# A gated mix of a spectral filter and a state-space layer: the spectral part moves into the matmul accumulation

## The chip, the cores and the metric

The kernel runs on one core of one Trainium2 chip. The metric is device time in microseconds (us). Three runs of the kernel before gave 412.79, 413.42 and 415.82 us, so the median is 413.42 us.

The core has five engines that run their own queues in order and wait for each other on semaphores: PE multiplies matrices into PSUM, DVE (vector) and ACT (scalar) work elementwise and read PSUM, POOL is hardly used here, and SP issues the transfers (DMAs).

## The reference

For x of 2048 rows by 1024 columns, with a gate g per row:

```
g = sigmoid((x * gate_w).sum(-1))
a = irfft2(rfft2(x) * (w_r + 1j*w_i))               # spectral part
b = 2*Re(C h) + x*Dskip,  h_t = Lam_bar h_{t-1} + B_bar x_t   # state-space part
out = g*a + (1-g)*b
```

The gate and `1-g` are rounded to bf16, and the output is bf16.

## The kernel before, in words

The output is made in 16 row tiles of 128 rows (`tb`). The state-space part works in 8 chunks of 256 rows (`c`), each in two halves of the state (`q`); such a half is a **unit** (L202). A unit multiplies x by B on PE (two blocks `psu` of 32 matmuls, L209), ACT casts each block into the tile `h` (L211), and DVE rotates, scans (L223) and rotates back (L215 to L234). The unit leaves `h` ready for the **C product** (`c_gemm`, L456): for a row tile, 16 matmuls of 512 columns from `h` (L462) and 4 small ones that add x*Dskip (L466), once for each half of the columns, into a tile `ps_y` of two PSUM banks.

The spectral part (`gfnet`, L240) runs between the units until about half of the span and leaves `ZT`. What is left of it for a row tile stands in `finish` (L477): 8 matmuls (L483) into `ps_id`, one ACT instruction that scales them by g into a piece of the buffer `raw` (L486), and four DVE additions and subtractions (L488, L489, L491, L492) that give g*a in a tile `ga`. Then DVE multiplies `ps_y` by 1-g and adds `ga` (L500), and SP sends the tile out (L501).

The first four row tiles have their C product done before the spectral part is ready. `early` (L470) scales it by 1-g on ACT and sends it to the scratch tensor `y_scratch` in two halves. `finish` without a `psy` fetches it again: for each half a load into the one buffer `yl` (L497) and a DVE addition (L498). These are the **late tiles** 0 to 3. The twelve others are own tiles 4 to 15.

The main loop (L663) makes chunks 4 to 7. Each of its 8 **halves** is a unit, the C product and `finish` of an own tile two chunks back, and, in the first four halves, `finish` of a late tile. After the loop the own tiles 12 to 15 remain (L670); this is the **tail**.

PSUM is full: two buffers of two banks for `ps_y` (pool `psA`), and two of two banks that `psu` and `ps_id` share (pool `psU`). The piece of `raw` that ACT writes is chosen by `tb % 2`, and so is the piece that L488 and L489 write. The tiles `ga` have two buffers. The scheduler reorders the program a little when it writes each engine's queue; on the chip the queues are strictly in order.

Of the kernel before, what the change touches and what calls it, by code (L numbers as in the profile page):

```python
# [11 lines left out]
ACT = mybir.ActivationFunctionType  # L12
ALU = mybir.AluOpType
FP32 = mybir.dt.float32
# [6 lines left out]
D = 1024  # L21
K = 512
H = K // 2
P = 128
# [60 lines left out]
def kernel(  # L85
# [17 lines left out]
    nc = tc.nc  # L103
    x = A_x[0]
    out2 = out[0]
# [15 lines left out]
    y_dram = dram.tile([NEARLY, 2, P, K], FP32, name="y_scratch")  # L121


    cpool = ctx.enter_context(tc.tile_pool(name="cpool", bufs=1, side="left"))
# [18 lines left out]
    ident = cpool.tile([P, P], BF16, name="ident")  # L143
# [53 lines left out]
    def halloc(shape, dtype):  # L197
        pool = hpool[hcount[0] % (NHA + NHB) >= NHA]
        hcount[0] += 1
        return pool.tile(shape, dtype, name="h")  # L200

    def unit(c, q):  # L202
        sh = [P, 2, 4, TC]
        u = halloc(sh, BF16)
        for ri in range(2):
            psu = psU.tile([P, 4, TC], FP32, name="psu", tag="psu")
            for j in range(4):
                for d8 in range(8):
                    nc.tensor.matmul(psu[:, j, :], lhsT=BT[4 * q + j][:, ri, d8, :],  # L209
                                     rhs=xT[:, d8, TC * c:TC * (c + 1)], start=(d8 == 0), stop=(d8 == 7))  # L210
            nc.scalar.copy(out=u[:, ri], in_=psu)  # L211
        js = slice(4 * q, 4 * q + 4)
        bc = lambda i: tab[:, i:i + 1, js, :].to_broadcast(sh)
        su = up.tile(sh, BF16, name="su")
        nc.vector.tensor_mul(out=su, in0=u[:, ::-1], in1=bc(1))  # L215
        nc.vector.tensor_mul(out=u, in0=u, in1=bc(0))  # L216
        nc.vector.tensor_add(out=u[:, 0], in0=u[:, 0], in1=su[:, 0])  # L217
        nc.vector.tensor_sub(out=u[:, 1], in0=su[:, 1], in1=u[:, 1])  # L218
        if c:
            nc.vector.tensor_add(out=u[:, :, :, 0], in0=u[:, :, :, 0], in1=carry[:, :, js])  # L220
        for ri in range(2):
            seg = u[:, ri].rearrange("p j t -> p (j t)")
            nc.vector.tensor_tensor_scan(out=seg, data0=rz[:, js].rearrange("p j t -> p (j t)"), data1=seg,  # L223
                                         initial=0.0, op0=ALU.mult, op1=ALU.add)
        if c + 1 < NCH:
            gl = u[:, :, :, TC - 1]
            nc.vector.tensor_mul(out=ck[:, 0, :, js], in0=gl, in1=cTC[:, js].unsqueeze(1).to_broadcast([P, 2, 4]))
            nc.vector.tensor_mul(out=ck[:, 1, :, js], in0=gl[:, ::-1], in1=sTC2[:, :, js])
            nc.vector.tensor_add(out=carry[:, :, js], in0=ck[:, 0, :, js], in1=ck[:, 1, :, js])
        sg = up.tile(sh, BF16, name="sg", tag="su")  # L230
        nc.vector.tensor_mul(out=sg, in0=u[:, ::-1], in1=bc(3))  # L231
        nc.vector.tensor_mul(out=u, in0=u, in1=bc(2))  # L232
        nc.vector.tensor_add(out=u[:, 0], in0=u[:, 0], in1=sg[:, 0])  # L233
        nc.vector.tensor_sub(out=u[:, 1], in0=u[:, 1], in1=sg[:, 1])  # L234
        hs[c, q] = u


    fft = {}
# [196 lines left out]
    def pull(budget):  # L435
        state["credit"] += budget
        while state["credit"] > 0 and not state["done"]:
            try:
                v = next(gen)
                if v == "ia":  # L440
                    after_ia()
                elif v == "ib":
                    after_ib()
                else:
                    state["credit"] -= v
            except StopIteration:
                state["done"] = True
# [5 lines left out]
            nc.sync.dma_start_transpose(out=CT[ri][:, :, P * q:P * (q + 1)], in_=src[P * q:P * (q + 1), :])  # L453


    def c_gemm(tb, pool=None, tag="ps"):  # L456
        c, tq = tb // 2, tb % 2
        psy = (pool or psA).tile([P, D], FP32, name="ps_y", tag=tag)
        for dh in range(2):
            for i in range(16):  # L460
                jb, ri = i // 2, i % 2
                nc.tensor.matmul(psy[:, 512 * dh:512 * (dh + 1)], lhsT=hs[c, jb // 4][:, ri, jb % 4, P * tq:P * (tq + 1)],  # L462
                                 rhs=CT[ri][:, jb, 512 * dh:512 * (dh + 1)], start=(i == 0), stop=False)
            for d4 in range(4):
                d8 = 4 * dh + d4
                nc.tensor.matmul(psy[:, P * d8:P * (d8 + 1)], lhsT=xT[:, d8, P * tb:P * (tb + 1)],  # L466
                                 rhs=fft["dgD"][:, d8, :], start=False, stop=(d4 == 3))
        return psy

    def early(tb):  # L470
        psy = c_gemm(tb, psU, "psu")
        for hf in range(2):
            ye = fft["gq"].tile([P, K], FP32, name="ye", tag="ga")
            nc.scalar.activation(out=ye, in_=psy[:, K * hf:K * (hf + 1)], func=ACT.Copy, scale=omg[:, tb:tb + 1])
            nc.sync.dma_start(out=y_dram[tb, hf], in_=ye)

    def finish(tb, psy=None):  # L477
        ZT_t = fft["ZT"]
        pse = psU.tile([P, 4, H], FP32, name="ps_id", tag="psu")
        for slot, (cls, ri) in enumerate(((0, 0), (1, 1), (0, 1), (1, 0))):  # L480
            for kb in range(2):
                i = 4 * cls + 2 * kb + ri
                nc.tensor.matmul(pse[:, slot, :], lhsT=ZT_t[:, i, tb, :], rhs=fft["Gi"][:, i, :],  # L483
                                 start=(kb == 0), stop=(kb == 1))
        part = raw[:, D * (2 + tb % 2):D * (3 + tb % 2)].rearrange("p (s c n) -> p s c n", s=2, c=2)
        nc.scalar.activation(out=part.rearrange("p s c n -> p (s c) n"), in_=pse, func=ACT.Copy, scale=gB[:, tb:tb + 1])  # L486
        eo = raw[:, D * (4 + tb % 2):D * (5 + tb % 2)].rearrange("p (c k) -> p c k", c=2)
        nc.vector.tensor_add(out=eo[:, :, 0:H], in0=part[:, 0], in1=part[:, 1])  # L488
        nc.vector.tensor_sub(out=eo[:, :, K - 1:H - 1:-1], in0=part[:, 0], in1=part[:, 1])  # L489
        ga = fft["gq"].tile([P, 2, K], BF16, name="ga")  # L490
        nc.vector.tensor_add(out=ga[:, 0], in0=eo[:, 0], in1=eo[:, 1])  # L491
        nc.vector.tensor_sub(out=ga[:, 1], in0=eo[:, 0], in1=eo[:, 1])  # L492
        o = ga.rearrange("p h n -> p (h n)")
        if psy is None:
            for hf in range(2):
                ye = fft["gq"].tile([P, K], FP32, name="yl", bufs=1)
                nc.sync.dma_start(out=ye, in_=y_dram[tb, hf])  # L497
                nc.vector.tensor_add(out=ga[:, hf], in0=ye, in1=ga[:, hf])  # L498
        else:
            nc.vector.scalar_tensor_tensor(out=o, in0=psy, scalar=omg[:, tb:tb + 1], in1=o, op0=ALU.mult, op1=ALU.add)  # L500
        nc.sync.dma_start(out=out2[P * tb:P * (tb + 1), :], in_=o)  # L501


    def turn_x(r):
# [71 lines left out]
    for r in range(16):  # L576
        if r >= 2:
            turn_x(r)
        for d8 in range(8):
            nc.tensor.matmul(zps[:, r:r + 1], lhsT=xT[:, d8, P * r:P * (r + 1)], rhs=gwT[:, d8:d8 + 1],  # L580
                             start=(d8 == 0), stop=(d8 == 7))
# [12 lines left out]
    raw = t3p.tile([P, 6 * D], BF16, name="raw")  # L594
# [38 lines left out]
    gB = cpool.tile([P, 16], FP32, name="gB")  # L633
    nc.vector.tensor_copy(out=gB, in_=g_bf)
    omg_bf = cpool.tile([P, 16], BF16, name="omg_bf")
    nc.vector.tensor_scalar(out=omg_bf, in0=g_bf, scalar1=-1.0, scalar2=1.0, op0=ALU.mult, op1=ALU.add)
    omg = cpool.tile([P, 16], FP32, name="omg")
    nc.vector.tensor_copy(out=omg, in_=omg_bf)
    pull(5.0)
    unit(0, 0)  # L640
    pull(7.5)
# [19 lines left out]
    todo = list(range(NEARLY, 16))  # L661
    late = list(range(NEARLY))
    for c in range(4, 8):  # L663
        for q in range(2):
            unit(c, q)
            tb = todo.pop(0)
            finish(tb, c_gemm(tb))
            if late:
                finish(late.pop(0))
    for tb in todo:  # L670
        finish(tb, c_gemm(tb))


# [28 lines left out]
```

## Time and profile before

| what | value |
|---|---|
| time of the three runs, median | 413.42 us |
| time of the profiled execution | 413.43 us |
| its span, first to last instruction | 411.6 us |
| busy PE, DVE, ACT in the span | 365.1, 307.8, 168.9 us |
| mean granted TensorE clock | 0.953 of full speed |

The profile is one execution. Its rows give times from the start of the span. A row "PE ... x32" is a run of instructions put together; the time in brackets is how long the engine stood idle before it, and what ended the wait. Matmuls are pipelined, so the rate of PE is read from the starts of two rows, not from the duration of one instruction.

### The profile page before, as it was taken

The numbers are of one execution on the slowest core, as the hardware profiler recorded it, in microseconds if no ns is written. First come the engines' busy times: TensorE is split into PE (matmuls) and PEld (weight loads), VectorE is DVE, ScalarE is ACT, GpSimd is POOL, SyncE is SP. The second block draws the span as 40 slices with busy tenths as digits, with TensorE's granted clock in tenths as the row PEclk, the third lists the DMA queues.
The fourth block names the chain that finished last, engine by engine and source line by source line (L and its number), as shares of the span: only waits on it lengthen the run. The fifth ranks groups of instructions, "written<-read, shape, count | busy, mean of one in ns | idle before, by whom it ended". The sixth has DMA issues, their size and how long they took to land. (4 is left out here: it accounts for less than half of the span.)

```text
span 411.6 us, 6481 instructions
## 1 busy us (share of the span) xinstructions
PE 365.1 (89%) x2601; PEld 239.7 (58%) x2601; DVE 307.8 (75%) x477; ACT 168.9 (41%) x210; POOL 28.8 (7%) x68
## 2 busy tenths in 40 slices
PE   4868998999797998999999988689796999999992
PEld 4836555667574454457766765556464767764551
DVE  2873598196989898990098897959696999999332
ACT  2759797664221588848721212121212113202111
POOL 7600011162000000000000000000000000000000
PEclk9879999999899699999999999969898999999997
DMA  7999921987742288659310103011111000000001
GB/s 207 340 201 208 212 77 53 223 191 148 179 146 79 82 274 314 225 173 292 123 53 2 51 2 100 3 51 51 53 51 53 25 27 2 25 27 16 36 32 45
DMA packets 58077, 45.84 MB, mean 111 GB/s; under 512 B 38720, under 2 KB 43200, under 8 KB 57792
## 3 DMA queue, kind: packets, MB, share of 16 engines
q1 hardware_dynamic: 57616, 45.41, 38.8%
q0 software_dynamic: 352, 0.02, 0.7%
q8 instruction: 20, 0.33, 0.3%
q14 instruction: 9, 0.07, 0.1%
q10 hardware_dynamic: 80, 0.01, 0.0%
HBM read 22.35 MB, written 14.69 MB: 90 GB/s over the span
## 5 line engine op out<-in xcount | busy, mean ns | idle before, releaser
L209 PE MATMUL psu<-xT,BT 128*128 128x256 bf16 x1024 | 129.3, 283 | 14.8 <-ACT raw L486 13.4
L209 PEld LDWEIGHTS <-BT 128*128 128x128 bf16 x1024 | 103.1, 101 | 38.8 <-issue 15.8
L462 PE MATMUL ps_y<-CT,h 128*128 128x512 bf16 x512 | 117.2, 379 | 0.7 <-DVE ga L500 0.7
L462 PEld LDWEIGHTS <-h 128*128 128x128 bf16 x512 | 49.5, 98 | 53.2 <-issue 0.9
L223 DVE TENSOR_TENSOR_SCAN h<-rz,h 128x1024 bf16<-128x1024 f32 x32 | 71.8, 2278 | 0.3
L486 ACT ACTIVATE raw<-ps_id,gB 128x1024 bf16<-128x1024 f32 x16 | 17.8, 1113 | 109.1 <-PE ps_id L483 85.5
L215 DVE TENSOR_TENSOR su<-h,tab 128x2048 bf16<-128x2048 bf16 x16 | 19.6, 1222 | 48.6 <-ACT h L211 48.5
L211 ACT CAST h<-psu 128x1024 bf16<-128x1024 f32 x32 | 32.3, 1010 | 57.1 <-PE psu L209 57.1
L249 PE MATMUL ps_fd<-G_sb,preT 128*128 128x512 bf16 x128 | 32.0, 397 | 4.7 <-ACT X L252 4.3
L249 PEld LDWEIGHTS <-preT 128*128 128x128 bf16 x128 | 18.6, 146 | 15.2 <-issue 8.5
L252 ACT CAST X<-ps_fd 128x1024 bf16<-128x1024 f32 x16 | 20.7, 1304 | 9.3 <-PE ps_fd L249 9.3
L359 ACT CAST X<-ps_s 128x1024 bf16<-128x1024 f32 x16 | 16.2, 1013 | 17.1 <-PE ps_s L357 17.1
L216 DVE TENSOR_TENSOR h<-h,tab 128x2048 bf16<-128x2048 bf16 x16 | 19.6, 1222 | 0.5
L488 DVE TENSOR_TENSOR raw<-raw 128x512 bf16<-128x512 bf16 x16 | 6.7, 418 | 17.3 <-ACT raw L486 17.3
L232 DVE TENSOR_TENSOR h<-h,tab 128x2048 bf16<-128x2048 bf16 x16 | 19.6, 1222 | 0.1
L231 DVE TENSOR_TENSOR sg<-h,tab 128x2048 bf16<-128x2048 bf16 x16 | 19.5, 1217 | 0.1
L507 PE MATMUL pt<-ident,BT 128*128 128x128 bf16 x128 | 12.8, 271 | 5.6 <-DMA BT<-in_A_x_dram 5.5
L380 ACT CAST C<-ps_is 128x1024 bf16<-128x1024 f32 x16 | 16.2, 1014 | 3.6 <-PE ps_is L378 3.2
L396 ACT CAST ZT<-ps_is 128x1024 bf16<-128x1024 f32 x16 | 16.1, 1012 | 3.0 <-PE ps_is L394 2.3
L392 PE MATMUL ps_is<-R_sb,raw 128*128 128x256 bf16 x64 | 14.8, 272 | 1.7 <-DMA raw<-turn_scratch 1.7
L500 DVE SCALAR_TENSOR_TENSOR ga<-ps_y,omg,ga 128x1024 bf16<-128x1024 f32 x12 | 15.4, 1283 | 1.2
L483 PE MATMUL ps_id<-raw,ZT 128*128 128x256 bf16 x128 | 15.9, 273 | 0.0
(188 smaller groups left out, 445.9 us busy)
## 6 DMA issues: line engine op xcount, KB each, us to landing
BT<-in_A_x_dram SPq DMA_DIRECT2D x8, 512.0 KB, 6.4
turn_scratch<-A SPq DMA_DIRECT2D x16, 256.0 KB, 2.9
Bb<-turn_scratch SPq DMA_DIRECT2D x16, 256.0 KB, 3.9
turn_scratch<-C SPq DMA_DIRECT2D x16, 256.0 KB, 3.1
raw<-turn_scratch SPq DMA_DIRECT2D x16, 256.0 KB, 5.3
out_dram<-ga SPq DMA_DIRECT2D x16, 256.0 KB, 2.0
W_b<-in_A_w_r_dram SPq DMA_DIRECT2D x16, 128.0 KB, 4.2
W_b<-in_A_w_i_dram SPq DMA_DIRECT2D x16, 128.0 KB, 3.8
```

The costliest lines, as they stand in the source:

```text
L209: nc.tensor.matmul(psu[:, j, :], lhsT=BT[4 * q + j][:, ri, d8, :], rhs=xT[:, d8, TC * c:TC * (c + 1)], start=(d8 == 0), stop=(d8 == 7))
L211: nc.scalar.copy(out=u[:, ri], in_=psu)
L215: nc.vector.tensor_mul(out=su, in0=u[:, ::-1], in1=bc(1))
L216: nc.vector.tensor_mul(out=u, in0=u, in1=bc(0))
L223: nc.vector.tensor_tensor_scan(out=seg, data0=rz[:, js].rearrange("p j t -> p (j t)"), data1=seg, initial=0.0, op0=ALU.mult, op1=ALU.add)
L231: nc.vector.tensor_mul(out=sg, in0=u[:, ::-1], in1=bc(3))
L232: nc.vector.tensor_mul(out=u, in0=u, in1=bc(2))
L249: nc.tensor.matmul(ps[:, cls, :], lhsT=preT_A[:, cls, d4, j, :], rhs=G_sb[:, cls, d4, :], start=(d4 == 0), stop=(d4 == 3))
L252: nc.scalar.copy(out=X1.rearrange("p r (i c) -> p c r i", c=2), in_=ps.rearrange("p c (r i) -> p c r i", r=2))
L359: nc.scalar.copy(out=X2, in_=ps2)
L462: nc.tensor.matmul(psy[:, 512 * dh:512 * (dh + 1)], lhsT=hs[c, jb // 4][:, ri, jb % 4, P * tq:P * (tq + 1)], rhs=CT[ri][:, jb, 512 * dh:51 ...
L486: nc.scalar.activation(out=part.rearrange("p s c n -> p (s c) n"), in_=pse, func=ACT.Copy, scale=gB[:, tb:tb + 1])
```

## The change

For an own tile the spectral part is scaled by g/(1-g) in place of g (`grat`, made once from `omg` by a reciprocal and a product on DVE; `omg` is kept above 2^-20). It is added to the C product in PSUM: for each half of the columns one more matmul of 512 columns with the identity as its weights and `ga` as its moving operand ends the accumulation. ACT then scales the sum by 1-g (two instructions of 512 columns) into `raw`, and the output leaves from there. DVE's L500 is gone for own tiles.

The order changes too. The spectral part of an own tile (`spectral`) now stands ahead of the unit of its half, and its C product behind the unit, as it was. The late tiles leave the main loop: in the tail, each of the four passes finishes one late tile, makes the spectral part of the next own tile, and then the C product of this one. `early` is as it was.

```diff
-    def c_gemm(tb, pool=None, tag="ps"):
+    def c_gemm(tb, pool=None, tag="ps", ga=None):
...
                 nc.tensor.matmul(psy[:, P * d8:P * (d8 + 1)], lhsT=xT[:, d8, P * tb:P * (tb + 1)],
-                                 rhs=fft["dgD"][:, d8, :], start=False, stop=(d4 == 3))
+                                 rhs=fft["dgD"][:, d8, :], start=False, stop=(d4 == 3 and ga is None))
+            if ga is not None:
+                nc.tensor.matmul(psy[:, 512 * dh:512 * (dh + 1)], lhsT=ident, rhs=ga[:, dh], start=False, stop=True)
         return psy
...
-    def finish(tb, psy=None):
+    def spectral(tb, scale):
...
-        nc.scalar.activation(out=part.rearrange("p s c n -> p (s c) n"), in_=pse, func=ACT.Copy, scale=gB[:, tb:tb + 1])
+        nc.scalar.activation(out=part.rearrange("p s c n -> p (s c) n"), in_=pse, func=ACT.Copy, scale=scale[:, tb:tb + 1])
...
-            nc.vector.scalar_tensor_tensor(out=o, in0=psy, scalar=omg[:, tb:tb + 1], in1=o, op0=ALU.mult, op1=ALU.add)
-        nc.sync.dma_start(out=out2[P * tb:P * (tb + 1), :], in_=o)
+        return ga
+
+    def late_tile(tb):
+        ga = spectral(tb, gB)
+        for hf in range(2):
+            ye = fft["gq"].tile([P, K], FP32, name="yl", bufs=1)
+            nc.sync.dma_start(out=ye, in_=y_dram[tb, hf])
+            nc.vector.tensor_add(out=ga[:, hf], in0=ye, in1=ga[:, hf])
+        nc.sync.dma_start(out=out2[P * tb:P * (tb + 1), :], in_=ga.rearrange("p h n -> p (h n)"))
+
+    def own_tile(tb, ga):
+        psy = c_gemm(tb, ga=ga)
+        o = raw[:, D * (2 + tb % 2):D * (3 + tb % 2)].rearrange("p (h n) -> p h n", h=2)
+        for hf in range(2):
+            nc.scalar.activation(out=o[:, hf], in_=psy[:, K * hf:K * (hf + 1)], func=ACT.Copy, scale=omg[:, tb:tb + 1])
+        nc.sync.dma_start(out=out2[P * tb:P * (tb + 1), :], in_=o.rearrange("p h n -> p (h n)"))
...
-    nc.vector.tensor_copy(out=omg, in_=omg_bf)
+    nc.vector.tensor_scalar_max(out=omg, in0=omg_bf, scalar1=float(2.0 ** -20))
+    grat = cpool.tile([P, 16], FP32, name="grat")
+    nc.vector.reciprocal(out=grat, in_=omg)
+    nc.vector.tensor_mul(out=grat, in0=grat, in1=gB)
...
     for c in range(4, 8):
         for q in range(2):
+            tb = todo.pop(0)
+            ga = spectral(tb, grat)
             unit(c, q)
-            tb = todo.pop(0)
-            finish(tb, c_gemm(tb))
-            if late:
-                finish(late.pop(0))
+            own_tile(tb, ga)
+    ga = spectral(todo[0], grat)
     for tb in todo:
-        finish(tb, c_gemm(tb))
+        late_tile(late.pop(0))
+        ga_next = spectral(tb + 1, grat) if tb + 1 < 16 else None
+        own_tile(tb, ga)
+        ga = ga_next
```

The queues show what the order of the code doesn't. First DVE's queue at the end of a unit in one of the first four halves, before the change; the first L489 to L500 are of the own tile, the second L488 to L498 of the late tile, and L215 begins the next unit:

```order
L234 TENSOR_TENSOR h<-h,sg 128x1024
L489 TENSOR_TENSOR raw<-raw 128x2x256
L491 TENSOR_TENSOR ga<-raw 128x512 [waits DMAHW3_49,DVE_49]
L492 TENSOR_TENSOR ga<-raw 128x512
L500 SCALAR_TENSOR_TENSOR ga<-ps_y,omg,ga 128x1024 [waits DVE_49,PE_49]
L488 TENSOR_TENSOR raw<-raw 128x2x256 [waits Activation_49]
L489 TENSOR_TENSOR raw<-raw 128x2x256
L491 TENSOR_TENSOR ga<-raw 128x512 [waits DMAHW5_49,DVE_49]
L492 TENSOR_TENSOR ga<-raw 128x512
L498 TENSOR_TENSOR ga<-yl,ga 128x512 [waits DMAHW6_49,DVE_49]
L215 TENSOR_TENSOR su<-h,tab 128x2048 [waits Activation_49]
L498 TENSOR_TENSOR ga<-yl,ga 128x512 [waits DMAHW0_49,DVE_49]
```

The same place in DVE's queue of the changed kernel (its L490, L491, L493, L494 are the four operations of the spectral part):

```order
L234 TENSOR_TENSOR h<-h,sg 128x1024
L490 TENSOR_TENSOR raw<-raw 128x2x256 [waits Activation_49]
L491 TENSOR_TENSOR raw<-raw 128x2x256
L493 TENSOR_TENSOR ga<-raw 128x512 [waits DVE_49,PE_49]
L494 TENSOR_TENSOR ga<-raw 128x512
L215 TENSOR_TENSOR su<-h,tab 128x2048 [waits Activation_49]
```

L500 and the work of the late tile have left DVE's queue between two units; L493 now waits for PE, which must have read the `ga` of two tiles ago.

Next PE's queue of the changed kernel around one tile's C product in the main loop. Weight loads (but one) and repeated matmuls are left out; L485 is the spectral matmul of the next own tile, L209 its half's unit:

```order
L462 MATMUL ps_y<-CT_789,h 128x512
...
L466 MATMUL ps_y<-dgD,xT 128x128
L469 LDWEIGHTS ident
L469 MATMUL ps_y<-ga,ident 128x512 [waits DVE_49]
...
L485 MATMUL ps_id<-raw,ZT 128x256 [waits Activation_49]
...
L209 MATMUL psu<-xT,BT_115 128x256 [waits Activation_49]
```

Before, no matmul of a C product waited for the spectral part; now the last matmul of each half of the columns waits for DVE, with the next spectral matmuls and the next unit queued behind it.

Last, DVE's queue of the changed kernel in the tail, from the late tile 0 (the first L502) to the own tile 13 (the last L493 and L494):

```order
L494 TENSOR_TENSOR ga<-raw 128x512
L502 TENSOR_TENSOR ga<-yl,ga 128x512 [waits DVE_49]
L490 TENSOR_TENSOR raw<-raw 128x2x256 [waits Activation_49]
L491 TENSOR_TENSOR raw<-raw 128x2x256
L502 TENSOR_TENSOR ga<-yl,ga 128x512 [waits DMAHW7_49,DVE_49]
L493 TENSOR_TENSOR ga<-raw 128x512 [waits DVE_49,PE_49]
L494 TENSOR_TENSOR ga<-raw 128x512
```

The `ga` of an own tile stands behind the second addition of the late tile, and so behind a load from `y_scratch`. On SP's queue there, the loads, the outputs of late tiles and the outputs of own tiles alternate.

## Rows read from the trace of the kernel before

**Rows 1.** Busy time by stretch: us, busy per engine (instructions), granted clock, DMA share, GB/s.

```profile
205.00:240.00 35.00, 35.00 (x246) 22.82 (x244) 30.76 (x34) 6.59 (x9) 0.00 (x0) 1.00 0.08 31
240.00:320.00 80.00, 66.58 (x456) 46.02 (x455) 65.30 (x97) 16.56 (x16) 0.00 (x0) 0.91 0.14 47
320.00:378.00 58.00, 58.00 (x412) 38.43 (x411) 56.77 (x69) 10.53 (x10) 0.00 (x0) 1.00 0.05 19
378.00:412.00 34.00, 25.65 (x152) 13.58 (x149) 12.59 (x22) 4.45 (x4) 0.00 (x0) 0.93 0.10 39
```

**Rows 2.** Waits, 205 to 412: who waited for whom, total us, times, longest.

```profile
ACT raw L486 <- DVE raw L489: 23.6, 4, 7.0
PE psu L209 <- ACT raw L486: 13.4, 4, 4.4
```

**Rows 3.** Timeline of one half with a late tile: start, us, what [idle before].

```profile
267.19 0.42 DVE L489 TENSOR_TENSOR raw<-raw 128x512 bf16<-128x512 bf16 x1
...
267.73 1.11 ACT L486 ACTIVATE raw<-ps_id,gB 128x1024 bf16<-128x1024 f32 x1 [6.96 <-DVE raw L489]
...
268.89 6.11 PE L209 MATMUL psu<-xT,BT 128*128 128x256 bf16 x32 [4.42 <-ACT raw L486]
...
276.08 1.22 DVE L215 TENSOR_TENSOR su<-h,tab 128x2048 bf16<-128x2048 bf16 x1 [4.23 <-ACT h L211]
```

**Rows 4.** Timeline: the same block of 32 matmuls after other waits.

```profile
248.17 3.65 PE L209 MATMUL psu<-xT,BT 128*128 128x256 bf16 x32 [2.44 <-ACT raw L486]
...
290.93 5.32 PE L209 MATMUL psu<-xT,BT 128*128 128x256 bf16 x32 [3.28 <-ACT raw L486]
```

**Rows 5.** Timeline of PE: a half without a late tile.

```profile
324.78 7.15 PE L209 MATMUL psu<-xT,BT 128*128 128x256 bf16 x64
...
331.77 3.62 PE L462 MATMUL ps_y<-CT,h 128*128 128x512 bf16 x16
...
335.22 0.39 PE L466 MATMUL ps_y<-dgD,xT 128*128 128x128 bf16 x4
...
339.12 1.04 PE L483 MATMUL ps_id<-raw,ZT 128*128 128x256 bf16 x8
...
340.00 7.15 PE L209 MATMUL psu<-xT,BT 128*128 128x256 bf16 x64
```

**Rows 6.** Timeline: where the main loop will begin.

```profile
219.38 1.23 DVE L215 TENSOR_TENSOR su<-h,tab 128x2048 bf16<-128x2048 bf16 x1 [1.72 <-ACT h L211]
...
225.49 7.15 PE L209 MATMUL psu<-xT,BT 128*128 128x256 bf16 x64
...
225.74 1.26 ACT L474 ACTIVATE ye<-ps_y,omg 128x512 f32<-128x512 f32 x2 [6.39 <-PE ps_y L466]
```

**Rows 7.** Timeline: one unit on DVE, and the cast ahead of it.

```profile
362.40 1.01 ACT L211 CAST h<-psu 128x1024 bf16<-128x1024 f32 x1 [2.48 <-PE psu L209]
...
364.25 1.22 DVE L215 TENSOR_TENSOR su<-h,tab 128x2048 bf16<-128x2048 bf16 x1
...
376.55 0.42 DVE L488 TENSOR_TENSOR raw<-raw 128x512 bf16<-128x512 bf16 x1
```

**Rows 8.** Timeline: PE after a short wait in the tail, and the end.

```profile
379.53 3.61 PE L462 MATMUL ps_y<-CT,h 128*128 128x512 bf16 x16 [0.72 <-DVE ga L500]
...
403.34 1.04 PE L483 MATMUL ps_id<-raw,ZT 128*128 128x256 bf16 x8
404.46 1.11 ACT L486 ACTIVATE raw<-ps_id,gB 128x1024 bf16<-128x1024 f32 x1 [7.11 <-PE ps_id L483]
405.61 0.42 DVE L488 TENSOR_TENSOR raw<-raw 128x512 bf16<-128x512 bf16 x1 [5.29 <-ACT raw L486]
...
407.26 1.28 DVE L500 SCALAR_TENSOR_TENSOR ga<-ps_y,omg,ga 128x1024 bf16<-128x1024 f32 x1
```

**Rows 9.** Timeline: a load of half a late tile, and the addition that waits for it.

```profile
251.21 0.32 SPq L497 DMA_DIRECT2D yl<-y_scratch  x1
...
253.91 0.69 DVE L498 TENSOR_TENSOR ga<-yl,ga 128x512 bf16<-128x512 f32 x1 [2.73 <-DMA yl<-y_scratch]
```

**Rows 10.** Line L389: loads of 256 KB each, at a DMA share of 0.81.

```profile
DMA to landing us min/median/max: 3.3/5.3/5.8
```

**Rows 11.** Lines L638 and L564: duration ns min/median/max, first and last start.

```profile
L638 DVE CAST omg<-omg_bf x1: 174/174/174, 28.6 to 28.6; 128x16 f32<-128x16 bf16 x1
...
L564 DVE RECIPROCAL inv<-den x1: 202/202/202, 8.7 to 8.7; 128x8 f32<-128x8 f32 x1
```

More of the change, by code (lines that the diff above doesn't have):

```diff
@@ L492, in finish @@
         nc.vector.tensor_sub(out=ga[:, 1], in0=eo[:, 0], in1=eo[:, 1])
[L493 to L499, printed above, removed]
-            nc.vector.scalar_tensor_tensor(out=o, in0=psy, scalar=omg[:, tb:tb + 1], in1=o, op0=ALU.mult, op1=ALU.add)
-        nc.sync.dma_start(out=out2[P * tb:P * (tb + 1), :], in_=o)
+        return ga
[12 more added lines that the diff above has]
+        nc.sync.dma_start(out=out2[P * tb:P * (tb + 1), :], in_=o.rearrange("p h n -> p (h n)"))
     def turn_x(r):
```

## The prediction

> **What bounds the kernel now.** I began with busy time by stretch, because the share over the whole span hides that the stretches differ. From 205 to 240 us PE never stops [rows 1]. From 240 to 320, the four halves with a late tile, PE is busy for 66.6 of 80 us at a mean granted clock of 0.91, and DVE for only 65.3. From 320 to 378, the four halves without one, PE is full again and DVE nearly so (56.8 of 58). So the first four halves are neither PE's nor DVE's limit, and the waits have to say what they are.
>
> The waits name a ring [rows 2]. ACT's scaling of a spectral part (L486) waits 23.6 us in four waits for DVE's L489, and PE's next unit block waits 13.4 us in four waits for that L486. The timeline shows one turn [rows 3]: L489 of the own tile stands on DVE's queue behind a whole unit and runs at 267.19; only then may ACT scale the late tile's part, which goes to the same piece of `raw` (tiles 4 and 0 have the same parity), at 267.73; and only when ACT has emptied that PSUM buffer may PE fill it with the unit's second block, at 268.89. PE has lost 4.42 us, ACT's cast comes late, and DVE then idles 4.23 us before L215. Each engine waits for the others in turn.
>
> The waits cost more than their length. The block after the 4.42 us wait takes 6.11 us for 32 matmuls [rows 3]; the same block after a wait of 2.44 us takes 3.65, and after one of 3.28 us 5.32 [rows 4]. The granted clock fell towards the lower of its two levels (1.2 of 2.4 GHz) after the longer waits.
>
> **PE's work, as it would run without waits.** From the starts in a half without a late tile [rows 5]: a unit's 64 matmuls take 331.77 - 324.78 = 6.99 us, a C product 339.12 - 331.77 = 7.35, a spectral part 340.00 - 339.12 = 0.88. In both kernels everything up to the C product of early tile 3 stands in the same order, so the main loop begins on PE at 225.49 [rows 6]. Before, PE then had 8 x (6.99 + 7.35) + 4 x 7.35 + 16 x 0.88 = 158.2 us of work, which would end at 383.7; it ended at 403.34 + 0.88 = 404.2 [rows 8]. So 20.5 us of waits and low clock lie there, 13.4 of them the waits on L486.
>
> **The change, part by part.**
> - *Identity matmuls, added:* 24 of 512 columns. The trace has none. The nearest row is the C product's own matmul of 512 columns, 16 of them in 335.22 - 331.77 = 3.45 us, 0.216 each [rows 5]. The other bound is that each stalls for a matmul's full 379 ns or so (3.62 us for 16 is from the first start to the last end, so 3.62 - 15 x 0.216 = 0.38). I take 0.216, as the identity's weights can load ahead as all others do: 0.43 a tile, 5.2 in all; the bound adds 3.9.
> - *The late tiles out of the main loop:* the own tiles that remain have alternating parity, so ACT's scaling no longer waits for DVE; the ring opens. A half is then 6.99 + 7.35 + 0.88 + 0.43 = 15.65 us of PE.
> - *L500 off DVE:* DVE's work in a half is a unit, 376.55 - 364.25 = 12.30 [rows 7], and four spectral operations, 407.26 - 405.61 = 1.65 [rows 8]: 13.95. That is below 15.65, so PE sets the pace, and DVE idles 1.7 us a half.
> - *The added wait, identity matmul for `ga`:* behind it on PE's queue stand the next spectral part and the next unit, so a late `ga` would hold everything. A unit's last cast ends 0.88 + 6.99 + 0.2 + 1.01 = 9.1 us into its half (0.2 and 1.01 from the cast in [rows 7]); DVE adds 12.30 and 1.65, so the next `ga` is ready at 23.05, 7.4 us into the next half. The identity matmul comes at 0.88 + 6.99 + 3.67 = 11.5. Slack 4.1. For the first half the unit begins at 219.38 [rows 6], `ga` is ready at 233.4, and the need is at 237.0. Slack 3.6. I cost the wait at nothing in the main loop; its cover is this slack.
> - *Output by ACT:* two instructions, 1.26 us together as in `early` [rows 6]; with the spectral scaling and two casts ACT has about 4.5 us a half. Nothing.
> - *Main loop:* 225.49 + 8 x 15.65 = 350.7.
> - *Tail, PE's work:* 4 x (7.35 + 0.43) + 8 x 0.88 = 38.2, to 388.9.
> - *Tail, waits:* the third spectral part needs the buffer of the first, which ACT empties only after tile 11's output: 350.7 + 0.25 + 1.26 + 1.14 = 353.4, while PE comes at 352.9: 0.5. Tile 12's `ga` follows the last unit: 335.05 + 9.1 + 12.30 + 1.65 = 358.1, while PE comes at 357.5: 0.6. Later ones have 2.5 us or more by the same reckoning. PE ends at 390.0.
> - *Late tiles in the tail:* each of a tile's two loads must wait for the addition before it, since `yl` has one buffer. Only the first load is early. Tile 0's parts are ready at 360.1, its first addition (0.69) ends at 360.8; seven loads of 2.70 [rows 9] and seven additions, three issues of an output between, end at 385.6. They stay under PE's work.
> - *End:* before, the last matmul was followed by ACT, five DVE operations, and 411.6 - (407.26 + 1.28) = 3.1 us for the output [rows 8]. Now it is 0.25 + 1.26 + 3.1 = 4.6, so the span ends at 394.6.
> - *Start:* two small operations more on DVE near 28.6 us, 0.20 and 0.17 by the nearest rows [rows 11]: 0 to 0.4 by whether DVE leads there. I take 0.2.
>
> **Sum:** a span of 394.8, against 411.6. In terms: 20.5 of waits gone, 1.1 of new ones, 5.2 of matmuls added, 2.8 saved at the end, 0.2 lost at the start. Time and span of the profiled execution differ by 413.43 - 411.6 = 1.8, and its time is that of the median, so I forecast **396.6 us**.
>
> **Rivals.**
> 1. *The clock falls in the tail.* Waits remain there, short but one or more in a pass. Against it: after a wait of 0.72 us the next 16 matmuls took 3.61 us [rows 8], as without one, and after 2.44 us the block was at full rate [rows 4]. If it fell once in each of four passes, at 5.32 - 3.65 = 1.7 to 6.11 - 3.65 = 2.5 us each, the time would be 403.3 to 406.4. The Trainium skill's "TensorE: Matmul & The Clock Gate", section "A second HAM failure mode: psum-queue depth-cycling", says that a PE that idles briefly but often between groups of matmuls can swing between its two clock levels. By that rule this rival would hold; the rows above speak against it. Chance 0.06.
> 2. *The late loads become the chain, and it is slower.* In the tail seven loads stand in series, and a late tile's second addition stands on DVE ahead of the next own tile's `ga`, so PE would wait as well. With L for a load, the last late output ends at 360.8 + 7 x (L + 0.69) + 1.0 + 3.1 = 369.7 + 7 L. It is hidden up to L = 3.6. Loads of the same 256 KB took 3.3 to 5.8 us earlier [rows 10], under a DMA share of 0.8, and at 5.8 the span would be 410.3, the time 412.1: nothing gained. Beyond 6.0 it is slower than before. For it: one queue carries loads and outputs in turn, and a load can stand behind an output that waits for ACT. Against it: the DMA share in the tail was 0.10 [rows 1], and the one load that was waited for took 2.7 us. Chance 0.13: 0.05 for 399 to 409, 0.04 within 1% of before, 0.04 slower.
> 3. *The ring closes elsewhere:* the identity matmul, behind DVE, takes the place of L486, so that PE waits in each half. It needs DVE to be 4 us later than the rows say. Even then DVE's own 13.95 a half is shorter than PE's 15.65, so the delay can't build up; once, it costs up to 4 us, and some clock: 398 to 403. Chance 0.06.
>
> **Numbers.** The forecast case has 0.75; its own range is 394.5 (no tail waits, a start that moves by a microsecond) to 400.5 (identity matmuls at their bound). The three rivals take the rest. The range of 8 in 10 is 394 to 403. A difference of about 1% (4 us) can be told from none. Faster by over 1%: 0.75 + 0.06 + 0.06 + 0.05 = 0.92; within 1%: 0.04; slower: 0.04.
>
> **What would show it.** PE full from 205 to about 390 at a granted clock of 1.00; unit blocks in the main loop 15.65 us apart; no wait of PE on ACT's scaling or on DVE but two of about half a microsecond after 350; DVE with a gap of some 1.7 us before each L215; additions of late tiles done by 386. A unit spacing above 16, or a wait of the identity matmul on DVE in the main loop, would refute the slack; a last late output behind the last own one would mean rival 2.

## The result

The changed kernel took 395.5 us (median; 393.05 to 396.38) against 414.1 for the kernel before, measured together with it: a ratio of 0.954, interval 0.948 to 0.960. Its profiled execution took 396.38 us with a span of 394.6. Forecast were 396.6 and 394.8, with a range of 394 to 403.

**Busy time by stretch**, columns as in [rows 1]:

```profile
205.00:240.00 35.00, 34.90 (x245) 22.94 (x243) 30.62 (x38) 7.59 (x10) 0.00 (x0) 1.00 0.09 31
240.00:320.00 80.00, 80.00 (x585) 55.16 (x583) 71.14 (x92) 21.58 (x26) 0.00 (x0) 1.00 0.05 18
320.00:351.00 31.00, 31.00 (x227) 21.38 (x226) 27.07 (x34) 8.46 (x10) 0.00 (x0) 1.00 0.05 18
351.00:390.00 39.00, 38.52 (x233) 21.23 (x231) 22.13 (x44) 13.42 (x16) 0.00 (x0) 1.00 0.30 95
390.00:395.00 5.00, 0.00 (x0) 0.00 (x0) 0.69 (x1) 1.26 (x2) 0.00 (x0) 0.77 0.28 105
```

From 240 to 320, where PE was busy for 66.58 us at a clock of 0.91, it is now full at 1.00. It stays so until 390, but for half a microsecond.

**PE's waits** from 205 to 395, columns as in [rows 2]. PE's line of [rows 2] is gone, and this is all that PE waits for. Of ACT's line one wait of 4.1 us is left, in the tail, with no wait of PE behind it.

```profile
PE ps_y L469 <- DVE ga L493: 0.2, 1, 0.2
PE ps_id L485 <- ACT raw L488: 0.2, 1, 0.2
```

**Timeline of the main loop** of the changed kernel, its first half and the start of the next two:

```profile
225.49 1.04 PE L485 MATMUL ps_id<-raw,ZT 128*128 128x256 bf16 x8
...
237.29 0.38 PE L469 MATMUL ps_y<-ga,ident 128*128 128x512 bf16 x1
237.50 3.62 PE L462 MATMUL ps_y<-CT,h 128*128 128x512 bf16 x16
...
241.39 1.04 PE L485 MATMUL ps_id<-raw,ZT 128*128 128x256 bf16 x8
...
249.01 0.42 DVE L494 TENSOR_TENSOR ga<-raw 128x512 bf16<-128x512 bf16 x1
...
250.50 1.23 DVE L215 TENSOR_TENSOR su<-h,tab 128x2048 bf16<-128x2048 bf16 x1 [1.07 <-ACT h L211]
...
252.93 0.38 PE L469 MATMUL ps_y<-ga,ident 128*128 128x512 bf16 x1
...
303.97 1.04 PE L485 MATMUL ps_id<-raw,ZT 128*128 128x256 bf16 x8
...
319.62 1.04 PE L485 MATMUL ps_id<-raw,ZT 128*128 128x256 bf16 x8
```

The loop begins at 225.49, as before [rows 6]. Halves are 319.62 - 303.97 = 15.65 us apart; only the first is longer, 241.39 - 225.49 = 15.90. An identity matmul takes 0.21 from start to start, and `ga` is there (249.43) 3.5 us before PE wants it (252.93).

**Timeline of the tail** of the changed kernel:

```profile
353.49 1.03 PE L485 MATMUL ps_id<-raw,ZT 128*128 128x256 bf16 x8 [0.24 <-ACT raw L488]
...
358.01 0.38 PE L469 MATMUL ps_y<-ga,ident 128*128 128x512 bf16 x1 [0.24 <-DVE ga L493]
...
372.61 0.69 DVE L502 TENSOR_TENSOR ga<-yl,ga 128x512 bf16<-128x512 f32 x1 [1.98 <-DMA yl<-y_scratch]
...
373.33 0.33 SPq L503 DMA_DIRECT2D out_dram<-ga  x1
...
375.48 0.42 DVE L493 TENSOR_TENSOR ga<-raw 128x512 bf16<-128x512 bf16 x1 [2.18 <-DMA out_dram<-ga]
...
377.88 0.69 DVE L502 TENSOR_TENSOR ga<-yl,ga 128x512 bf16<-128x512 f32 x1
...
389.62 0.38 PE L469 MATMUL ps_y<-ga,ident 128*128 128x512 bf16 x1
390.09 1.26 ACT L509 ACTIVATE raw<-ps_y,omg 128x512 bf16<-128x512 f32 x2 [6.39 <-PE ps_y L469]
390.14 0.69 DVE L502 TENSOR_TENSOR ga<-yl,ga 128x512 bf16<-128x512 f32 x1 [2.80 <-DMA yl<-y_scratch]
390.86 0.33 SPq L503 DMA_DIRECT2D out_dram<-ga  x1
391.38 0.33 SPq L510 DMA_DIRECT2D out_dram<-raw  x1
```

The last late addition ends at 390.83, its output is issued half a microsecond ahead of the last own one. The forecast had it done by 385.6.

### The profile page after: what moved, and what is told of

Read it like the earlier page. It is cut to its first block, busy times and chain, and to the rows that moved or that the text cites. A ratio compares the mean times of both kernels' runs of the same rounds, so it can differ in the third digit from the quotient of the medians.

```text
span 394.6 us, 6556 instructions
## 1 busy us (share of the span) xinstructions
PE 363.6 (92%) x2625; PEld 239.6 (61%) x2625; DVE 294.2 (75%) x467; ACT 183.0 (46%) x234; POOL 28.8 (7%) x68
## 4 chain that ended last, share of the span: by engine, by line
PE 61%; DVE 13%; DMA 11%; ACT 7%; SPq 3%; issue 3%; POOLq 1%; POOL 0%; ACTq 0%; DVEq 0%
PE ps_y L462 23%; PE psu L209 21%; PE ps_fd L249 5%; ACT X L252 3%; DMA Bb<-turn_scratch 3%; DMA raw<-turn_scratch 3%; DMA BT<-in_A_x_dram 3%; PE ps_id L485 3%; DVE h L223 2%; PE ps_y L466 2%; PE ps_is L392 1%; PE ps_y L469 1%; DMA W_b<-in_A_w_i_dram 1%; PE ps_is L394 1%; DMA BT<-in_B_B_re_dram 1%
## 5 line engine op out<-in xcount | busy, mean ns | idle before, releaser
L209 PE MATMUL psu<-xT,BT 128*128 128x256 bf16 x1024 | 123.1, 276 | 1.0 <-DMA BT<-in_B_B_re_dram 0.9
L209 PEld LDWEIGHTS <-BT 128*128 128x128 bf16 x1024 | 100.7, 99 | 20.9 <-issue 1.6
L215 DVE TENSOR_TENSOR su<-h,tab 128x2048 bf16<-128x2048 bf16 x16 | 19.6, 1225 | 48.4 <-ACT h L211 48.2
L509 ACT ACTIVATE raw<-ps_y,omg 128x512 bf16<-128x512 f32 x24 | 15.2, 683 | 67.9 <-PE ps_y L469 67.9
L249 PE MATMUL ps_fd<-G_sb,preT 128*128 128x512 bf16 x128 | 31.1, 388 | 4.7 <-ACT X L252 4.3
L359 ACT CAST X<-ps_s 128x1024 bf16<-128x1024 f32 x16 | 16.2, 1013 | 17.1 <-PE ps_s L357 17.1
L380 ACT CAST C<-ps_is 128x1024 bf16<-128x1024 f32 x16 | 16.2, 1014 | 3.5 <-PE ps_is L378 3.1
L488 ACT ACTIVATE raw<-ps_id,grat 128x1024 bf16<-128x1024 f32 x12 | 13.4, 1113 | 7.8 <-DMA out_dram<-raw 7.8
L485 PE MATMUL ps_id<-raw,ZT 128*128 128x256 bf16 x128 | 16.1, 272 | 0.2 <-ACT raw L488 0.2
L267 POOL COPY Acol<-A 128x2 bf16<-128x2 bf16 x16 | 9.9, 619 | 68.6 <-DVE A L266 35.7
```

Source lines behind the costliest of these rows:

```text
L249: nc.tensor.matmul(ps[:, cls, :], lhsT=preT_A[:, cls, d4, j, :], rhs=G_sb[:, cls, d4, :], start=(d4 == 0), stop=(d4 == 3))
```

## The experiments

Three theories. **A**, the prediction's: late tiles close a ring, DVE's L489 to ACT's scaling to PE's block, by the parity of `raw`; the late tiles' leaving opens it. **B**: DVE simply has too much to do, and L500's leaving is what pays. **C**, formed after the first four runs: in the first four halves DVE's queue is a second limit beside the ring, about as long as it, made by the late tile's operations and by the wait for the one load buffer `yl`. Ratios are to the kernel before, measured together with each.

### One part alone: the late tiles, the addition in PSUM

*Late only:* the kernel before, with its late tiles in the tail.

```diff
             finish(tb, c_gemm(tb))
-            if late:
-                finish(late.pop(0))
     for tb in todo:
+        finish(late.pop(0))
         finish(tb, c_gemm(tb))
```

> The kernel before with one part of the change: the late tiles leave the main loop and are finished in the tail, one ahead of each own tile. The spectral part is still added by DVE (L500) behind the C product; there are no identity matmuls. Theory A (the time was lost in the ring of the main loop: ACT's scaling of the late tile waits for DVE, PE waits for ACT, the clock falls): the ring is gone here as well, a half costs the larger of PE's 6.99 + 7.35 + 0.88 = 15.2 us and DVE's 12.30 + 1.65 + 1.28 = 15.2 us, so the main loop ends at about 225.5 + 8 x 15.3 = 348 us, the tail adds 4 x 8.23 + 4 x 0.88 = 36.4 us of PE and 7.4 us of end, and the time is 392 to 397 us, equal to the changed kernel or a little below it. Theory B (the time was lost because DVE had too much to do, and it is the 1.28 us of L500 a tile that pays): at least 400 us, since L500 is still there.

391.8 us, 0.948 [0.943, 0.953]. This is just below A's 392 to 397. The stretch of the first four halves in this run:

```profile
240.00:320.00 80.00, 80.00 (x599) 56.64 (x597) 78.40 (x102) 16.70 (x16) 0.00 (x0) 1.00 0.05 18
```

PE is full with L500 still on DVE, which is itself busy for 78.4 of 80 us. B falls: the move alone gives all of the gain.

*PSUM only:* the changed kernel, with the late tiles back in the main loop.

```diff
             own_tile(tb, ga)
+            if late:
+                late_tile(late.pop(0))
...
     for tb in todo:
-        late_tile(late.pop(0))
```

> The changed kernel with its other part alone: the addition in PSUM, the output by ACT and the spectral part ahead of the unit stay, but the late tiles are finished in the first four halves of the main loop, behind the own tile, as before. Theory A: the ring comes back in another form, since the late tile's scaling again needs a piece of raw and a PSUM buffer that its half's own tile holds, so waits of PE on ACT's scaling of 2 us or more a half return, and the time is 402 to 412 us. Theory B (DVE's load): DVE has 12.30 + 2 x 1.65 + 1.37 = 17.0 us in each of these halves and 13.95 in the others, so the main loop takes 4 x 17.0 + 4 x 15.65 = 131 us, the tail 34.6 us, and the time is 397 us with hardly a wait of PE on ACT.

400.9 us, 0.971 [0.964, 0.979]. The same stretch, and DVE in one half, from a late tile's second addition over L215, the first operation of a unit, to the next L215:

```profile
240.00:320.00 80.00, 77.51 (x578) 54.96 (x577) 70.34 (x102) 26.36 (x29) 0.00 (x0) 1.00 0.16 54
```

```profile
253.53 0.69 DVE L502 TENSOR_TENSOR ga<-yl,ga 128x512 bf16<-128x512 f32 x1 [2.11 <-DMA yl<-y_scratch]
254.13 1.22 DVE L215 TENSOR_TENSOR su<-h,tab 128x2048 bf16<-128x2048 bf16 x1
...
272.57 1.22 DVE L215 TENSOR_TENSOR su<-h,tab 128x2048 bf16<-128x2048 bf16 x1
```

PE waited for no scaling of ACT here: the new order had opened the ring without the late tiles' leaving. What is left is DVE's pace, 272.57 - 254.13 = 18.4 us a half with 2.1 of it a wait for a load, while PE needs 16.6 (from the starts of two unit blocks, 244.56 and 261.19). The lag ends in four waits of the identity matmul for `ga`, 5.2 us in all. A's wait of PE on ACT did not come. B had DVE set the pace, but at 17.0 us a half, without the wait for the load.

### The ring alone

*Other piece:* in the kernel before, a late tile uses the other piece of `raw`, so ACT's scaling need not wait for the own tile's L489.

```diff
-        part = raw[:, D * (2 + tb % 2):D * (3 + tb % 2)].rearrange("p (s c n) -> p s c n", s=2, c=2)
+        pc = (tb + (psy is None)) % 2
+        part = raw[:, D * (2 + pc):D * (3 + pc)].rearrange("p (s c n) -> p s c n", s=2, c=2)
...
-        eo = raw[:, D * (4 + tb % 2):D * (5 + tb % 2)].rearrange("p (c k) -> p c k", c=2)
+        eo = raw[:, D * (4 + pc):D * (5 + pc)].rearrange("p (c k) -> p c k", c=2)
```

> The kernel before with one edit: the late tile uses the other piece of raw, so that ACT's scaling of it no longer waits for DVE's second operation on the own tile of the same half. Order, work and engines are as before. Theory A: the waits of PE's unit block on that scaling (13.4 us in four waits) shrink below 3 us in all, the clock stays up, and the four halves go from 21.2 us to DVE's own 12.30 + 2 x 1.65 + 1.28 + 1.37 = 18.3 us: 402 to 406 us. Theory B (DVE's load alone sets these halves, the ring only fills its idle time): 411 to 415 us.

409.8 us, 0.991 [0.987, 0.995]. DVE in one half, then two stretches, then two lines of the waits (L499 and L501 of this kernel are L498 and L500 of the kernel before):

```profile
251.64 0.69 DVE L499 TENSOR_TENSOR ga<-yl,ga 128x512 bf16<-128x512 f32 x1 [2.79 <-DMA yl<-y_scratch]
252.25 1.22 DVE L215 TENSOR_TENSOR su<-h,tab 128x2048 bf16<-128x2048 bf16 x1
...
272.47 1.22 DVE L215 TENSOR_TENSOR su<-h,tab 128x2048 bf16<-128x2048 bf16 x1
```

```profile
240.00:320.00 80.00, 80.00 (x594) 56.17 (x593) 68.70 (x101) 19.61 (x20) 0.00 (x0) 1.00 0.16 50
350.00:385.00 35.00, 23.94 (x119) 11.60 (x117) 25.73 (x33) 3.34 (x3) 0.00 (x0) 0.85 0.06 23
```

```profile
PE ps_y L462 <- DVE ga L501: 12.7, 3, 6.7
DVE ga L499 <- DMA yl<-y_scratch: 10.7, 4, 3.5
```

The ring is gone: PE is full from 240 to 320 at a clock of 1.00. Yet the time hardly moves, and A's 402 to 406 is missed. PE, running freely, takes 16.2 us a half (unit blocks start at 240.22, 256.41, 272.61), DVE 272.47 - 252.25 = 20.2 with 2.8 of it a wait for the load. The other halves are like it: from one L501 to the next DVE takes 20.3, 20.2, 19.1 and 20.5 us. DVE falls behind by 4 us a half, and from 350 on PE stands waiting for it, at a clock of 0.85. A full PE in a stretch is no gain if what it runs ahead of is the limit. C was formed here.

### The second limit, with the ring open and closed

*Piece and loads:* the other piece, and the parked products kept in bf16 so that two load buffers fit. *Loads only:* the second of these edits alone.

```diff
-    y_dram = dram.tile([NEARLY, 2, P, K], FP32, name="y_scratch")
+    y_dram = dram.tile([NEARLY, 2, P, K], BF16, name="y_scratch")
...
-            ye = fft["gq"].tile([P, K], FP32, name="ye", tag="ga")
+            ye = fft["gq"].tile([P, K], BF16, name="ye", tag="ga")
...
-                ye = fft["gq"].tile([P, K], FP32, name="yl", bufs=1)
+                ye = fft["gq"].tile([P, K], BF16, name="yl", bufs=2)
```

> The kernel before, with two edits: the late tile's spectral part uses the other piece of raw (as in the run of that edit alone, 409.8 us), and the parked products of the early tiles are kept in bf16 (they are rounded once more) so that two load buffers fit. The late tiles stay in the main loop and the mixing instruction stays on DVE. Theory C (DVE's queue is the limit in the first four halves, with its wait for the one load buffer): no addition waits 2.7 us for a load, DVE needs 12.30 + 2 x 1.65 + 1.28 + two additions of at most 0.69, about 17.7 to 18.3 us in a half where the edit of the piece alone had 20.3, so 4 x (2 to 2.6), 8 to 10 us less: 399 to 402 us. Theory A (once the ring through raw is open nothing but PE is left): no further gain, 408 to 411.

> The kernel before, with the parked products of the early tiles in bf16 (rounded once more) and two load buffers; the piece of raw is chosen as before, so the ring stands. Theory A (the ring is the cause, the loads are not): ACT's scaling still waits for the own tile's operations behind the unit, 411 to 414 us, no change. Theory C: both edits take time off the same turn, and since the ring still makes the late tile's scaling wait for DVE, the loads alone are worth 4 x 0 to 2.7 us: 403 to 413, and what they save is more with the ring open than with it closed.

| | one load buffer, fp32 | two, bf16 |
|---|---|---|
| ring closed | 1 (the kernel before) | 408.9 us, 0.990 [0.986, 0.994] |
| ring open | 409.8 us, 0.991 [0.987, 0.995] | 398.2 us, 0.964 [0.958, 0.969] |

Either edit alone is worth some 4 us (0.9% and 1.0% of 413), both together 15. Timeline of *loads only*, one turn:

```profile
245.86 3.65 PE L209 MATMUL psu<-xT,BT 128*128 128x256 bf16 x32 [2.45 <-ACT raw L486]
...
264.98 5.32 PE L209 MATMUL psu<-xT,BT 128*128 128x256 bf16 x32 [2.81 <-ACT raw L486]
```

```profile
250.60 1.23 DVE L215 TENSOR_TENSOR su<-h,tab 128x2048 bf16<-128x2048 bf16 x1 [1.65 <-ACT h L211]
...
271.38 1.23 DVE L215 TENSOR_TENSOR su<-h,tab 128x2048 bf16<-128x2048 bf16 x1 [3.37 <-ACT h L211]
```

Timeline of *piece and loads*, one turn of DVE (L499 are both additions of a late tile), and its stretch:

```profile
249.33 0.75 DVE L499 TENSOR_TENSOR ga<-yl,ga 128x512 bf16<-128x512 bf16 x2
250.00 1.22 DVE L215 TENSOR_TENSOR su<-h,tab 128x2048 bf16<-128x2048 bf16 x1
...
266.21 0.75 DVE L499 TENSOR_TENSOR ga<-yl,ga 128x512 bf16<-128x512 bf16 x2
266.88 1.22 DVE L215 TENSOR_TENSOR su<-h,tab 128x2048 bf16<-128x2048 bf16 x1
```

```profile
240.00:320.00 80.00, 80.00 (x595) 56.25 (x594) 79.00 (x119) 19.71 (x19) 0.00 (x0) 1.00 0.12 40
```

With the loads out of the way the ring still makes a turn of 20.8 us (271.38 - 250.60), and what DVE saved turns into idle time before L215. With the ring open, DVE's queue with its load wait makes one of 20.2. With both gone a turn is 16.9 us (266.88 - 250.00), without idle time. So two loops of nearly one length ran side by side, and opening one shows the other. C is borne out, if a little low in its gain (399 to 402 expected); A alone would have had 408 to 411 for both edits. The bf16 edit changes the load wait and the additions (0.75 in place of 1.3 for the pair) together, so their shares of the last 3.3 us stand as the trace has them, 2.8 and 0.5. It also halves the bytes of a load, so what the wait owes to the second buffer and what to the smaller load is not told apart.

### What the identity matmuls cost

*No identity:* the changed kernel without its 24 identity matmuls (own tiles leave the spectral part out of the sum).

```diff
-            if ga is not None:
-                nc.tensor.matmul(psy[:, 512 * dh:512 * (dh + 1)], lhsT=ident, rhs=ga[:, dh], start=False, stop=True)
```

> The changed kernel without the 24 identity matmuls; own tiles leave out the spectral part. Theory A (PE sets the pace from 225 us on, and each identity matmul costs it 0.216 us, its weights loaded ahead): 5.2 us less than the changed kernel, and up to 0.5 us more where PE waited for DVE: 389.5 to 391 us, with a half at 15.22 us. Rival (an identity matmul costs its own 0.38 us, or a wait for DVE hides in it): 9 us or more less, 386 us or below.

389.4 us, 0.943 [0.938, 0.948], 6.1 us below the changed kernel's first median, which was measured apart from it. The predicted price was 5.2, its bound 9.1; the starts in the main loop, 0.21 us apart, say the former, and so does the comparison from the main loop on (163.7 against 168.9 us, below).

### The loads in the tail

*Loads twice:* in the changed kernel each late load is issued twice, the second behind the first.

```diff
             nc.sync.dma_start(out=ye, in_=y_dram[tb, hf])
+            nc.sync.dma_start(out=ye, in_=y_dram[tb, hf])
```

> The changed kernel, with each load of a late half issued twice, one after the other into the same buffer, so that a load takes twice as long. Rival 2 of the prediction (the chain of loads, additions and outputs on SP's queue sets the end as soon as a load is slow): in the changed kernel the last late addition ended at 390.8, only half a microsecond ahead of what the end needs, so seven doubled loads of 2.6 to 2.9 us end some 18 to 20 us later: 412 to 416 us. The prediction's reckoning, by which loads of up to 3.6 us are hidden and 5.6 us would give 369.7 + 7 x 5.6 = 408.9 of span: 409 to 412. If PE's work hid them: under 400.

411.2 us, 0.996 [0.993, 1.000]: nearly the whole gain is gone, at the 409 to 412 of the prediction's formula (a span of 408.9 for L = 5.6; it was 408.7). From one late addition to the next it is 6.1 to 6.8 us, where the formula has 6.3. The end of that run:

```profile
399.52 0.32 SPq L501 DMA_DIRECT2D yl<-y_scratch  x1
402.08 0.32 SPq L502 DMA_DIRECT2D yl<-y_scratch  x1
404.85 0.69 DVE L503 TENSOR_TENSOR ga<-yl,ga 128x512 bf16<-128x512 f32 x1 [5.36 <-DMA yl<-y_scratch]
```

Rival 2's mechanism is real; only its condition, slow loads, was not met. The formula fits here, though it had the undoubled loads' end 5 us too early (385.6 for 390.83): with loads this long, the outputs that DVE waits for land while a load is under way.

*Four buffers:* in the changed kernel the late loads go to four slices of `rz`, which is free by then, so none waits for an addition. It was measured on one chip together with three earlier kernels.

```diff
-            ye = fft["gq"].tile([P, K], FP32, name="yl", bufs=1)
-            nc.sync.dma_start(out=ye, in_=y_dram[tb, hf])
+            ye = late_y(tb, hf)
             nc.vector.tensor_add(out=ga[:, hf], in0=ye, in1=ga[:, hf])
+            if tb + 2 < NEARLY:
+                nc.sync.dma_start(out=ye, in_=y_dram[tb + 2, hf])
```

> The changed kernel, with the late loads into four buffers (two slices each of rz, which is free after the last scan), so that no load waits for an addition. The prediction costed the late tiles at nothing because they stay under PE's work; the trace of the changed kernel had them end at 390.83, half a microsecond ahead of what the end needs. If they really stay hidden: 0 to 1 us less than the changed kernel of the same call, while the last late addition ends some 5 us or more earlier (the landing of a late tile's output, for which DVE waits 2.2 us each time, may keep part of the chain). If the chain held the end back: 2 to 4 us less.

394.0 us, 0.956 [0.952, 0.961], 1.0 us below the changed kernel there (395.1); the intervals overlap. No load is waited for any more; this is what is left:

```profile
DVE ga L493 <- DMA out_dram<-ga: 9.5, 3, 5.3
```

```profile
382.98 1.29 DVE L505 TENSOR_TENSOR ga<-rz,ga 128x512 bf16<-128x512 f32 x2
```

The late tiles end at 384.3, 3.4 us before PE's last matmul (387.33 + 0.38). From the end of the main loop they took 35.7 us (348.6 to 384.3), in the changed kernel 39.9 (350.9 to 390.8). So their loads' series is worth 4 us, and all of it was hidden in the changed kernel, with half a microsecond to spare: there too the last own output left as soon as ACT had scaled it (391.38, after 390.09 + 1.26). What DVE waits for in the chain now is mostly this: a late tile's output must land before DVE may write the next `ga`.

### The version put together, and the four on one chip

*Put together:* late tiles in the tail with four load buffers, DVE mixing as before but into `raw`, the spectral part ahead of the C product in the tail, and no addition in PSUM.

```diff
+    def mix(tb, psy, ga, split):
...
+            nc.vector.scalar_tensor_tensor(out=o[:, sl], in0=psy[:, sl], scalar=omg[:, tb:tb + 1], in1=g[:, sl],
+                                           op0=ALU.mult, op1=ALU.add)
...
     for tb in todo:
+        late_tile(late.pop(0))
+        ga_next = spectral(tb + 1) if tb + 1 < 16 else None
+        mix(tb, c_gemm(tb), ga, 1 if tb < 15 else 2)
+        ga = ga_next
```

> A version put together from what the runs showed: late tiles in the tail, no addition in PSUM (DVE mixes, as in the run with the late tiles alone, 391.8 us), the mixed tile is written into raw, in the tail the spectral part stands ahead of the C product, and the late loads have four buffers (two slices each of rz, which is free then), so they do not stand in series. Nothing is left out. Theory C: PE's 158.2 us from the main loop's start at 225.5 end at 383.7; then a mix in two pieces (1.3), an output (3.1) and 0.25 between: span 388.4, time 388 to 391, about 2 below the late tiles alone and 5 to 6 below the changed kernel. If the chain of loads was not what the end of that run waited for: 391 to 393, no gain.

390.1 us, 0.944 [0.940, 0.948]. Its end:

```profile
383.63 0.39 PE L466 MATMUL ps_y<-dgD,xT 128*128 128x128 bf16 x4
384.05 1.41 DVE L514 SCALAR_TENSOR_TENSOR raw<-ps_y,omg,ga 128x512 bf16<-128x512 f32 x2 [3.40 <-PE ps_y L466]
```

PE ends at 384.0, close to the 383.7 that the prediction gave for its work before the change without waits, though its main loop began 0.9 us earlier (224.63) and it waited once, 0.7 us. The repeats:

> The changed kernel once more, on one chip together with the late tiles alone, the version put together and the one with four landing buffers, so that differences of 1% can be told. The times so far, each against the kernel before (ratios 0.954, 0.948 and 0.944), say that the changed kernel is the slowest of these. Theory C: 395 to 397 us, ratio 0.950 to 0.960.

> The kernel before with only the late tiles moved to the tail, once more. Theory C (DVE's queue is relieved by that move alone, the addition in PSUM then only adds 5.2 us of PE work, 1.3 to 2 us of which the shorter end gives back): 3 to 4 us below the changed kernel of the same call, interval without overlap. Theory B (the addition in PSUM is what pays): no shorter than the changed kernel.

> The version put together, once more: 5 to 6 us below the changed kernel of the same call, 1 to 3 below the late tiles alone.

| on one chip, 5 rounds | us | ratio |
|---|---|---|
| the change | 395.1 | 0.958 [0.954, 0.963] |
| the change, four load buffers | 394.0 | 0.956 [0.952, 0.961] |
| late tiles alone | 392.8 | 0.953 [0.948, 0.958] |
| put together | 390.0 | 0.946 [0.942, 0.951] |

Only the version put together stands clear of the change. Late only and the change overlap here, so their difference is smaller than I expected: over all ten runs of each the medians are 392.3 and 395.3.

Much of the scatter lies ahead of the main loop, where the two parts of the change alter next to nothing. The scaling of early tile 3 by ACT, at the main loop's beginning, marks the point in each profile: the changed kernel twice, then late only twice.

```profile
225.74 1.26 ACT L476 ACTIVATE ye<-ps_y,omg 128x512 f32<-128x512 f32 x2 [6.39 <-PE ps_y L466]
224.16 1.26 ACT L476 ACTIVATE ye<-ps_y,omg 128x512 f32<-128x512 f32 x2 [6.39 <-PE ps_y L466]
223.03 1.26 ACT L474 ACTIVATE ye<-ps_y,omg 128x512 f32<-128x512 f32 x2 [6.39 <-PE ps_y L466]
224.83 1.26 ACT L474 ACTIVATE ye<-ps_y,omg 128x512 f32<-128x512 f32 x2 [6.39 <-PE ps_y L466]
```

| profiled executions | from that start to the end of the span, us |
|---|---|
| the change, twice | 394.6 - 225.74 = 168.9; 392.9 - 224.16 = 168.7 |
| the change, four load buffers | 392.1 - 223.44 = 168.7 |
| the change without identity matmuls | 387.6 - 223.93 = 163.7 |
| late tiles alone, twice | 388.3 - 223.03 = 165.3; 390.1 - 224.83 = 165.3 |
| put together, twice | 388.6 - 224.88 = 163.7; 388.8 - 225.13 = 163.7 |

Two profiles of one kernel agree within 0.2 us here. So once the late tiles are gone, the addition in PSUM, with its order and its output by ACT, costs 3.5 us; the identity matmuls cost 5.1 to 5.2, and the four load buffers give nothing that shows. The version put together is 1.6 ahead of the late tiles alone; which of its edits gives that was not run apart.

## Why the prediction was right, and where it was not

**The sum held, term by term.** The main loop's start (225.49), its spacing (15.65), the identity matmul (0.21 for 0.216), the slack of `ga` (3.5 us left of 4.1) and DVE's gap before L215 (1.1 to 1.6 for 1.7) are as reckoned or near it. The tail's two waits are where they were expected, 0.24 each for 0.5 and 0.6; the first half's extra 0.25 makes up for part of that. PE's last matmul ends at 390.00, the very figure forecast, and 4.6 us follow it. That the main loop began at the same 225.49 as in the kernel before is luck, for in the other profile of the changed kernel it began 1.6 earlier. The stretch from ACT's scaling of early tile 3 (225.74) to the end is not: the forecast's 394.6 - 225.74 is 168.9, and 168.9 and 168.7 were measured. The 0.2 for the start is not to be seen in this run.

**The cause was half told.** The step "the late tiles out of the main loop: the ring opens" took the ring for all that held the first four halves, since these were "neither PE's nor DVE's limit". The runs showed two loops, each about 20 to 21 us a half, and the ring alone is worth 4 us, not 20.5. The number came out right because the sum did not subtract the waits: it rebuilt PE's and DVE's work a half in the new order, and the late tile's operations and load waits had left DVE's queue as well. Had the change only opened the ring, the same argument would have said 402 to 406, and 409.8 was measured. What misled me was [rows 1]: DVE busy 65.3 of 80 looked like room. Of the 14.7 us idle, the ring itself made 10.8 (three waits for ACT's cast before L215), and only one wait was for `yl`:

```profile
DVE ga L498 <- DMA yl<-y_scratch: 2.7, 1, 2.7
```

The ring hid the others. With it open (*other piece*) a late tile's addition waits for its load in every half, four times and 10.7 us in all, so a profile with the ring in it doesn't show what DVE's turn will be without it.

**The addition in PSUM is no gain of its own here.** By the prediction's own terms it adds 5.2 of matmuls and 0.5 of waits (measured) and saves 2.8 at the end, a net 2.9; the two kernels differ by 2.9 over ten runs, and by 3.5 from the main loop on. Where the late tiles stay (*PSUM only*) the addition and the new order together are worth 12 us: PE no longer waits for ACT's scaling, and L500 has left a queue that is the limit. How much each of the two gives was not timed apart.

**The late tiles' end was mis-sized:** 385.6 forecast, 390.83 measured. The step took a load and an addition, 3.4 us, from each addition to the next. Within a tile that holds (3.5, but 4.6 in the second tile), but from one late tile to the next it is 4.4 once and 5.3 twice, as in 377.88 - 372.61: DVE waits 2.2 for the output of the tile before to land, as `ga` has two buffers, and then has the next own tile's operations to do. The step put that landing at nothing. It cost nothing, by half a microsecond.

**Rival 1 did not come.** The granted clock was 1.00 from 205 to 390 over the two short waits. In *PSUM only* PE waited four times, 1.7 us at most and 5.2 in all, and the clock from 240 to 378 was 1.00 too. The Trainium skill's "TensorE: Matmul & The Clock Gate", section "A second HAM failure mode: psum-queue depth-cycling", by which frequent short idling swings the clock, is not borne out by these waits; whether more frequent ones would do it, no run here shows.

## What to carry to other kernels

When two engines wait for each other in a ring, don't price its removal by the waits in the profile. Rebuild each engine's turn, its waits for loads included, as it will stand without the ring: the longest of them is the new pace, and it may be nearly as long as the old one. When a change has two parts, time each alone: here one gave all of it, and the other took a little back. An addition moved into PSUM, with the order that goes with it, paid here where the elementwise engine was a limit; where PE was, it cost its full matmul time, less what it took off the end.

## What the runs showed of the hardware

- Consecutive DVE instructions overlap: in *piece and loads* five operations of 0.42 us start 0.34 apart (262.67 to 264.01). So its turn took 16.9 where the durations of its instructions add up to 18.3.
- After a wait of 2.45 us PE's next 32 matmuls took 3.65 us, after one of 2.81 us 5.32 (*loads only*, above). In the kernel before it was 2.44 and 3.65, 3.28 and 5.32 [rows 4]. The granted clock from 240 to 320 was 0.94 and 0.91 of full speed.
- The scaling of early tile 3 by ACT, at the main loop's beginning, started between 223.03 (*late only*) and 225.79 (*PSUM only*) in the profiled executions, at 225.74 and 224.16 in two of the changed kernel. Differences below 3 us between single profiled runs mean little, unless they are read from that point on, where two profiles of a kernel agree within 0.2 us.
